# Gathering ten tiles ahead, score bursts set by the gather's position, smaller loads on more steps, and an FFN that runs on into the next batch

## The chip, the cores and the metric

The kernel runs on one core of one Trainium2 chip. The metric is the device time of one execution in microseconds: 660.77 us in the median of four runs of the kernel before (656.48 to 662.66). The engines named below are TensorE (PE; its weight loads are listed as PEld), VectorE (DVE), ScalarE (ACT), GpSimd (POOL) and SyncE (SP), which here only issues DMAs.

## The reference

Attention whose heads are mixed twice ("talking heads"), and then a feed-forward network with a squared ReLU. Batch 8, 12 heads, 448 positions, 64 values per head; the network is 768 to 2048 to 768 over all 3584 tokens. Inputs and output are float32.

```python
scores = scale * np.matmul(q, k.transpose(0, 1, 3, 2))
scores = np.einsum('bhij,hg->bgij', scores, w_pre)
attn = softmax(scores)                       # over the last axis
attn = np.einsum('bhij,hg->bgij', attn, w_post)
x = np.matmul(attn, v)                       # heads back to 768 columns
out = np.maximum(x @ w_in, 0.0) ** 2 @ w_out
```

## The kernel before

Everything is computed in bfloat16 with float32 sums. The 448 query rows of a batch are cut into 45 tiles of ten rows (the last has eight). For one tile, the scores of ten rows and twelve heads make 120 partitions by 448 keys; both head mixings are matmuls over these 120 partitions.

**Scores and the gather.** The scores of a batch are made in four blocks (12, 12, 12 and 9 tiles). A block is 128 query rows, and its tile `S` holds them row by partition: 128 x 12 heads x 448. `score_burst` (L264) makes half a block: six matmuls into six of the eight PSUM banks, then six copies into `S`, half on ScalarE (L279) and half on VectorE (L281). There are two `S` buffers, so a block's copies overwrite the block two before it. `gather` (L286) then moves ten rows from `S` into a tile `G` with 120 partitions, by a DMA that SP issues (L293). It needs the whole block, since each gather reads all heads. `G` has `AHEAD + 2` buffers.

**A step.** One tile is one step, and all batches run as one row of 360 steps (L371). In step i: `mix` (L296) multiplies `G` with the first mixing matrix (L299), ScalarE takes exp and its row sums (L302), VectorE the reciprocal (L304), and GpSimd scales to `d` (L306). `unmix` (L310) of the tile four steps back (`LAG`) does the second mixing and the transposition in four matmuls (L319), copied out by VectorE (L321). Then the gather of tile i + `AHEAD` is issued. The `exp` tile has three buffers.

**Other units on TensorE.** `turn_unit` (L133) transposes four heads of q or k of a batch and copies them to `qT` or `kT` on VectorE (L147). A batch has six such units. `bias_unit` (L153) and `av_unit` (L164) make the values' part; an `av` unit ends in three ScalarE activations (L179), and there are two for each third of a batch. A batch's feed-forward network is 16 FFN1 units (`ffn1_unit`, L207: six matmuls, ReLU on ScalarE L214, square on GpSimd L215) and 14 FFN2 units (`ffn2_unit`, L230: matmuls, a copy on VectorE for each second unit, stores issued by SP). The ReLU's tile `hr` has two buffers.

**What sets the order.** PE and POOL are under a manual schedule: their order is the order in which the loop emits. Two kinds of unit are put between the steps. Timed units stand in a table by step (`at_step`). FFN units stand in a list, `filler`. Each unit has a price in ns, written by hand. `fill(share)` is called twice in a step; it adds `share` to a balance and emits units until the balance is used up:

```python
rest = NT - (s0[1] if s0 else 0)
share = sum(w for w, _ in filler) / max(rest - 1, 1) / 2 if s0 else 1e9
...
for w, f in now:
    f()
    owed[0] -= w
fill(share)
```

So timed units are charged to the same balance. A batch's FFN units enter the list in step 5 of the next batch, and `rest` makes them end with that batch's last step; in steps 0 to 4 the list is empty. The turns of the next batch stand in steps 20 and 35, bias in step 20, `av` units in steps 20, 35 and 5 of the next batch. Score bursts of the next block stand in tile steps 0 and 4 of a block (0 and 2 of the short one).

**Loads.** GpSimd issues them (they cast to bfloat16): v, k and q of a batch as one DMA each (672 KB as landed) and each weight in four DMAs (768 KB), at steps of the table `loads`. The staging tiles of q and k have one buffer each, v has two. Only the first batch's q and k are loaded by four heads (224 KB).

**The start.** Three rounds, each of which turns four heads of k and q and makes their scores for block 0; then block 1; then the first six gathers.

Of the kernel before, what the change touches and what calls it, by code (L numbers as in the profile page):

```python
# [30 lines left out]
LAG = 4  # L31
AHEAD = 6
SCALE = 1.0 / 8.0
# [4 lines left out]
def kernel(  # L38
# [93 lines left out]

    def turn_unit(b, which, u):  # L133

        store, name = (qTs, "qT") if which == 0 else (kTs, "kT")
        if b not in store:
            store[b] = work.tile([P, NPAIR, S], BF16, name=name, tag=name, bufs=2)
        src = staged[b][which]
        ps = bank("tr_ps", BF16)
        for y in range(2):  # L140
            p = 2 * u + y
            for r in range(R):
                c = S * y + PR * r
                for hh in range(2):
                    nc.tensor.transpose(ps[64 * hh:64 * hh + 64, c:c + PR], src[0:PR, 2 * p + hh, r, :],  # L145
                                        ident[0:PR, 0:PR])
        nc.vector.tensor_copy(out=store[b][:, 2 * u:2 * u + 2, :],  # L147
                              in_=ps[:, 0:2 * S].rearrange("p (y s) -> p y s", y=2))

# [34 lines left out]

    def load_v(b):
        vs[b] = stage_tile("v", 2)
        load(vs[b], v, b)

    def load_k(b):
        kst = stage_tile("kst", 1)  # L190
        load(kst, k, b)
        staged[b] = (stage_tile("qst", 1), kst)

    def load_q(b):
        load(staged[b][0], q, b)

    def load_w1(x):
        n = DFF // 4
        nc.gpsimd.dma_start(out=w1[x][:, :, :],
                            in_=moe_w_in[:, n * x:n * x + n].rearrange("(c p) f -> p c f", p=P))  # L200

    def load_w2(x):
        n = DFF // 4
        nc.gpsimd.dma_start(out=w2[x][:, :, :],
                            in_=moe_w_out[n * x:n * x + n, :].rearrange("(c p) m -> p c m", p=P))
# [137 lines left out]
    with tc.manual_schedule(engines={PE, POOL}):  # L343
        first = turn_units(0)
        for x in range(3):
            first[2 * x][1]()
            first[2 * x + 1][1]()
            score_burst(0, 0, [2 * x, 2 * x + 1])
        for x in range(2):
# [8 lines left out]

        at_load(0, load_v, 0)
        at_load(2, load_k, 1)  # L360
        at_load(5, load_q, 1)
        for x in range(4):
            at_load(10 + 5 * x, load_w1, x)
            at_load(44 + 4 * x, load_w2, x)
        for b in range(B):
            if b + 1 < B:
                at_load(NT * b + 32, load_v, b + 1)
            if b + 2 < B:
                at_load(NT * b + 36, load_k, b + 2)
                at_load(NT * b + 40, load_q, b + 2)  # L370
        for i in range(len(steps) + LAG):  # L371
# [4 lines left out]
            if s0:  # L376
                b, t = s0
                blk, tl = divmod(t, TPB)
                if t == 0:
# [3 lines left out]
                    if b + 1 < B:  # L383
                        for x, u in enumerate(turn_units(b + 1)):
                            at_step(i + 16 + LAG if x < 3 else i + 31 + LAG, u)
            rest = NT - (s0[1] if s0 else 0)
            share = sum(w for w, _ in filler) / max(rest - 1, 1) / 2 if s0 else 1e9
            now = timed.pop(i, [])
# [14 lines left out]
            if i + AHEAD < len(steps):  # L403
                gather(steps[i + AHEAD])
            if s0:
                nxt = blocks.index((b, blk)) + 1
                first = [0, 4] if blk < 3 else [0, 2]
                if 1 < nxt < len(blocks) and tl in first:
                    x = first.index(tl)
                    score_burst(*blocks[nxt], [3 * x, 3 * x + 1, 3 * x + 2])  # L410
# [36 lines left out]
```

The softmax here doesn't subtract the row's maximum and nothing guards it: scores larger than these inputs give would overflow.

## Time and profile before

| | |
|---|---|
| median of four runs | 660.77 us |
| the profiled execution's own time | 662.66 us |
| its span, first to last instruction | 660.8 us |
| first mix / last mix (start) | 21.9 / 612.6 us |
| mean granted TensorE clock | 0.954 |
| first FFN1 unit | 109.3 us |
| last FFN, after the last mix's steps | 618.8 to 656.2 us |
| moved by DMA | 73.47 MB, of it 49.57 on the queue of SP and 22.81 on that of GpSimd |

The profile is of one execution, so sums in its durations are compared with 662.66, not with the median. A group's row gives busy time, the mean of one instruction, and then the idle time of that engine just before these instructions with what ended it. Matmuls are pipelined: the mean of one is longer than what it costs in a packed row. Idle time of an engine that isn't the bound costs nothing.

### The profile page before, as it was taken

The numbers are of one execution on the slowest core, as the hardware profiler recorded it, in microseconds if no ns is written. First come the engines' busy times: TensorE is split into PE (matmuls) and PEld (weight loads), VectorE is DVE, ScalarE is ACT, GpSimd is POOL, SyncE is SP. The second block draws the span as 40 slices with busy tenths as digits, with TensorE's granted clock in tenths as the row PEclk, the third lists the DMA queues.
The fourth block names the chain that finished last, engine by engine and source line by source line (L and its number), as shares of the span: only waits on it lengthen the run. The fifth ranks groups of instructions, "written<-read, shape, count | busy, mean of one in ns | idle before, by whom it ended". The sixth has DMA issues, their size and how long they took to land.

```text
span 660.8 us, 16952 instructions
## 1 busy us (share of the span) xinstructions
PE 606.0 (92%) x6282; PEld 375.5 (57%) x6282; DVE 422.6 (64%) x1029; ACT 405.1 (61%) x1193; POOL 374.7 (57%) x531
## 2 busy tenths in 40 slices
PE   4588758999899998999899999999899999999897
PEld 3245525666556655656556655656556665656554
DVE  3367656656676777677676778677676668665201
ACT  2567547755687548765687548765587549864330
POOL 3445456774387536774387536774377537763350
PEclk9668759999899999999999999999899999999899
DMA  9699999558744785349744695349744645433002
GB/s 127 101 190 198 164 153 196 108 73 134 162 73 80 128 141 121 73 73 152 161 88 80 120 151 126 67 73 158 162 79 72 109 96 109 77 68 95 23 0 84
DMA packets 90039, 73.47 MB, mean 111 GB/s; under 512 B 5476, under 2 KB 86884, under 8 KB 89956
## 3 DMA queue, kind: packets, MB, share of 16 engines
q1 hardware_dynamic: 51842, 49.57, 34.4%
q0 software_dynamic: 37984, 22.81, 26.0%
q8 instruction: 49, 0.80, 0.5%
q14 instruction: 34, 0.28, 0.1%
q10 hardware_dynamic: 130, 0.01, 0.0%
HBM read 45.63 MB, written 11.01 MB: 86 GB/s over the span
## 4 chain that ended last, share of the span: by engine, by line
PE 72%; DMA 17%; ACT 3%; DVE 3%; issue 2%; SPq 1%; POOL 1%; ACTq 0%; DVEq 0%; POOLq 0%
PE h_ps L210 22%; PE o_ps L237 19%; DMA G<-S 14%; PE m_ps L299 9%; PE at_ps L319 9%; PE ot_ps L171 5%; PE s_ps L274 5%; PE tr_ps L145 2%; DMA out_dram<-osb 2%; ACT e_sb L302 2%; DVE at L321 1%; SPq L293 1%; DMA qst<-in_q_dram 1%; PE vs_ps L158 1%; ACT S L279 1%
## 5 line engine op out<-in xcount | busy, mean ns | idle before, releaser
L306 POOL TENSOR_SCALAR d<-e_sb,rc 120x448 bf16<-120x448 f32 x360 | 228.4, 638 | 248.7 <-DVE rc L304 247.1
L321 DVE CAST at<-at_ps 112x480 bf16<-112x480 f32 x360 | 230.0, 651 | 99.3 <-PE at_ps L319 97.0
L302 ACT ACTIVATE e_sb<-m_ps 120x448 f32<-120x448 f32 x360 | 196.8, 555 | 130.2 <-PE m_ps L299 115.1
L299 PE MATMUL m_ps<-G,pre 120*120 120x448 bf16 x360 | 137.6, 382 | 29.9 <-DMA G<-S 25.5
L210 PE MATMUL h_ps<-xt,w 128*128 128x448 bf16 x768 | 164.7, 353 | 0.3
L237 PE MATMUL o_ps<-w,h 128*128 128x384 bf16 (+1 forms) x1024 | 162.5, 327 | 0.0
L319 PEld LDWEIGHTS <-d 120*128 120x128 bf16 (+1 forms) x1440 | 112.1, 102 | 55.4 <-issue 9.7
L319 PE MATMUL at_ps<-post,d 120*128 120x120 bf16 (+1 forms) x1440 | 139.2, 221 | 4.5 <-POOL d L306 3.7
L215 POOL TENSOR_TENSOR h<-hr 128x448 bf16<-128x448 f32 x128 | 119.2, 932 | 14.8 <-ACT hr L214 14.8
L237 PEld LDWEIGHTS <-h 128*128 128x128 bf16 (+1 forms) x1024 | 86.6, 101 | 52.4 <-issue 3.2
L210 PEld LDWEIGHTS <-w 128*128 128x128 bf16 x768 | 73.3, 98 | 60.7 <-issue 5.9
L281 DVE CAST S<-s_ps 128x448 bf16<-128x448 f32 x184 | 103.5, 616 | 4.8 <-PE s_ps L274 2.8
L279 ACT CAST S<-s_ps 128x448 bf16<-128x448 f32 x200 | 94.4, 553 | 15.7 <-PE s_ps L274 15.7
L214 ACT ACTIVATE hr<-h_ps 128x448 f32<-128x448 f32 x128 | 69.7, 544 | 47.9 <-PE h_ps L210 46.7
L304 DVE RECIPROCAL rc<-sm 120x1 f32<-120x1 f32 x360 | 56.8, 159 | 53.3 <-ACT e_sb L302 50.4
L299 PEld LDWEIGHTS <-pre 120*120 120x120 bf16 x360 | 49.1, 137 | 68.3 <-DMA G<-S 38.1
L302 ACT ACTIVATION_READ_ACCUMULATOR e_sb<-m_ps 120x1 f32 x360 | 76.7, 213 | 0.0
L179 ACT ACTIVATE xt<-ot_ps,bvec 128x150 bf16<-128x150 f32 (+1 forms) x144 | 42.9, 391 | 37.4 <-PE ot_ps L171 37.4
L274 PE MATMUL s_ps<-kT,qT 64*128 64x448 bf16 x384 | 60.3, 377 | 5.8 <-DVE qT L147 2.2
L244 DVE COPY osb<-o_ps 128x384 f32<-128x384 f32 x48 | 26.7, 557 | 51.5 <-PE o_ps L237 51.5
L171 PE MATMUL ot_ps<-at,v 112*64 112x150 bf16 x1152 | 48.2, 246 | 3.2 <-issue 2.0
L171 PEld LDWEIGHTS <-v 112*64 112x64 bf16 x1152 | 44.1, 121 | 5.6 <-issue 4.7
(33 smaller groups left out, 158.4 us busy)
## 6 DMA issues: line engine op xcount, KB each, us to landing
G<-S SPq DMA_DIRECT2D x352, 105.0 KB
v<-in_v_dram POOLq DMA_DIRECT2D x8, 672.0 KB, 10.7
kst<-in_k_dram POOLq DMA_DIRECT2D x7, 672.0 KB, 10.8
qst<-in_q_dram POOLq DMA_DIRECT2D x7, 672.0 KB, 13.6
w<-in_moe_w_in_dram POOLq DMA_DIRECT2D x4, 768.0 KB, 10.7
w<-in_moe_w_out_dram POOLq DMA_DIRECT2D x4, 768.0 KB, 10.7
out_dram<-osb SPq DMA_DIRECT2D x8, 336.0 KB
out_dram<-osb SPq DMA_DIRECT2D x8, 288.0 KB
```

What stands on the lines that cost most here:

```text
L171: nc.tensor.matmul(ps[64 * hh:64 * hh + 64, TQ * y:TQ * y + TQ], lhsT=vs[b][0:PR, g, r, :], rhs=at[0:PR, r, g, :], start=(y == 0 and r == ...
L210: nc.tensor.matmul(ps[:, 0:S], lhsT=w1[ft // 4][:, c2, ft % 4 * 128:ft % 4 * 128 + 128], rhs=xts[b][:, c2, :], start=(c2 == 0), stop=(c2 = ...
L215: nc.gpsimd.tensor_tensor(out=h2[:, :], in0=hr[:, :], in1=hr[:, :], op=ALU.mult)
L237: nc.tensor.matmul(dst, lhsT=h2ts[(b, ft)][:, mt * 128:mt * 128 + ROWS[mt]], rhs=w2[ft // 4][:, ft % 4, n2 * 384:(n2 + 1) * 384], start=(f ...
L274: nc.tensor.matmul(ps[:, 0:S], lhsT=qTs[b][rs, p, BLK_START[blk]:BLK_START[blk] + P], rhs=kTs[b][rs, p, :], start=True, stop=True)
L279: nc.scalar.copy(out=sb[:, h, :], in_=ps[:, 0:S])
L281: nc.vector.tensor_copy(out=sb[:, h, :], in_=ps[:, 0:S])
L299: nc.tensor.matmul(ps[0:n, 0:S], lhsT=pre[0:n, 0:n], rhs=Gs.pop(s)[0:n, :], start=True, stop=True)
L302: nc.scalar.activation(out=e[0:n, :], in_=ps[0:n, 0:S], func=ACT.Exp, scale=SCALE, accum_out=sm[0:n, 0:1])
L306: nc.gpsimd.tensor_scalar(out=d[0:n, 0:S], in0=e[0:n, :], scalar1=rc[0:n, 0:1], scalar2=-1.0 / S, op0=ALU.mult, op1=ALU.add)
L319: nc.tensor.matmul(ps[:, RG * r:RG * r + RG], lhsT=d[0:n, PR * r:PR * r + P], rhs=post[0:n, :], start=True, stop=True)
L321: nc.vector.tensor_copy(out=ats[(b, third)][0:PR, :, :, IQ * tl:IQ * tl + IQ], in_=ps[0:PR, 0:R * RG].rearrange("p (r g i) -> p r g i", r= ...
```

## The change

- `AHEAD` goes from 6 to 10: ten gathers before the first step, tile i + 10 in step i, and 12 `G` buffers.
- A score burst is emitted by the position of the gather, not of the mix: when the gather is at tile 2 and tile 6 of a block (2 and 5 of the short one), the next block's bursts follow. In steps, both bursts of a block come eight steps earlier than before (eight and seven where the short block precedes).
- q, k and v are loaded by four heads, the weights by half quarters, one piece a step, two steps apart or three. Batch 1's q and k come first, then v of batch 0, then the weights; batch 2's q and k partly move behind the first batch's end. From batch 1 on, q and k of the batch after next stand on steps 22 to 32 and the next v on 34 to 38.
- The turns: three now in step 16 (batch 0), 12 (batch 1) or 5 (later), the other three in step 20. At the start the copy of q goes to ScalarE, and the scores of a round are made one round later.
- `rest` now counts to step 5 of the next batch, so that FFN units are spread over 45 steps, from step 6 to step 5 of the batch after.

```diff
@@ -29,7 +29,7 @@
 TT = 15
 TQ = TT * IQ
 LAG = 4
-AHEAD = 6
+AHEAD = 10
 SCALE = 1.0 / 8.0
 ROWS = [128, 128, 128, 64]
 
@@ -130,7 +130,7 @@
                 out=cgblk[64 * hh:64 * hh + 64, :],
                 in0=ps[64 * hh:64 * hh + 64, 0:H].rearrange("p (c t) -> p t c", t=2)[:, hh, :], scalar1=1.0 / S)
 
-    def turn_unit(b, which, u):
+    def turn_unit(b, which, u, eng=None):
 
         store, name = (qTs, "qT") if which == 0 else (kTs, "kT")
         if b not in store:
@@ -144,8 +144,8 @@
                 for hh in range(2):
                     nc.tensor.transpose(ps[64 * hh:64 * hh + 64, c:c + PR], src[0:PR, 2 * p + hh, r, :],
                                         ident[0:PR, 0:PR])
-        nc.vector.tensor_copy(out=store[b][:, 2 * u:2 * u + 2, :],
-                              in_=ps[:, 0:2 * S].rearrange("p (y s) -> p y s", y=2))
+        (eng or nc.vector.tensor_copy)(out=store[b][:, 2 * u:2 * u + 2, :],
+                                       in_=ps[:, 0:2 * S].rearrange("p (y s) -> p y s", y=2))
 
     def turn_units(b):
         return [(430, lambda u=u, w=w: turn_unit(b, w, u)) for u in range(NPAIR // 2) for w in (1, 0)]
@@ -182,26 +182,30 @@
     def av_units(b, third):
         return [(800, lambda cp=cp: av_unit(b, third, cp)) for cp in range(2)]
 
-    def load_v(b):
-        vs[b] = stage_tile("v", 2)
-        load(vs[b], v, b)
-
-    def load_k(b):
-        kst = stage_tile("kst", 1)
-        load(kst, k, b)
-        staged[b] = (stage_tile("qst", 1), kst)
-
-    def load_q(b):
-        load(staged[b][0], q, b)
+    def load_v(b, x):
+        if x == 0:
+            vs[b] = stage_tile("v", 2)
+        load(vs[b], v, b, 4 * x, 4 * x + 4)
+
+    def load_qk(b, x):
+        if x == 0:
+            kst = stage_tile("kst", 1)
+            staged[b] = (stage_tile("qst", 1), kst)
+        u, w = x // 2, 1 - x % 2
+        load(staged[b][w], k if w else q, b, 4 * u, 4 * u + 4)
 
     def load_w1(x):
         n = DFF // 4
-        nc.gpsimd.dma_start(out=w1[x][:, :, :],
-                            in_=moe_w_in[:, n * x:n * x + n].rearrange("(c p) f -> p c f", p=P))
+        h = NPAIR // 2
+        c = x % 2 * h
+        nc.gpsimd.dma_start(out=w1[x // 2][:, c:c + h, :],
+                            in_=moe_w_in[128 * c:128 * c + 128 * h, n * (x // 2):n * (x // 2) + n].rearrange(
+                                "(c p) f -> p c f", p=P))
 
     def load_w2(x):
-        n = DFF // 4
-        nc.gpsimd.dma_start(out=w2[x][:, :, :],
+        n = DFF // 8
+        c = x % 2 * 2
+        nc.gpsimd.dma_start(out=w2[x // 2][:, c:c + 2, :],
                             in_=moe_w_out[n * x:n * x + n, :].rearrange("(c p) m -> p c m", p=P))
 
     def ffn1_unit(b, ft):
@@ -341,11 +345,12 @@
     blocks = [(b, blk) for b in range(B) for blk in range(4)]
     steps = [(b, t) for b in range(B) for t in range(NT)]
     with tc.manual_schedule(engines={PE, POOL}):
-        first = turn_units(0)
-        for x in range(3):
-            first[2 * x][1]()
-            first[2 * x + 1][1]()
-            score_burst(0, 0, [2 * x, 2 * x + 1])
+        for x in range(4):
+            if x < 3:
+                turn_unit(0, 1, x)
+                turn_unit(0, 0, x, nc.scalar.copy)
+            if x > 0:
+                score_burst(0, 0, [2 * x - 2, 2 * x - 1])
         for x in range(2):
             score_burst(0, 1, [3 * x, 3 * x + 1, 3 * x + 2])
         for x in range(AHEAD):
@@ -356,18 +361,22 @@
         def at_load(i, f, *args):
             loads.setdefault(i, []).append(lambda: f(*args))
 
-        at_load(0, load_v, 0)
-        at_load(2, load_k, 1)
-        at_load(5, load_q, 1)
-        for x in range(4):
-            at_load(10 + 5 * x, load_w1, x)
-            at_load(44 + 4 * x, load_w2, x)
-        for b in range(B):
+        for x in range(6):
+            at_load(2 * x, load_qk, 1, x)
+            at_load([40, 42, 44, 46, 55, 57][x], load_qk, 2, x)
+        for x in range(3):
+            at_load(12 + 2 * x, load_v, 0, x)
+            at_load(49 + 2 * x, load_v, 1, x)
+        for x in range(8):
+            at_load(18 + 3 * x, load_w1, x)
+            at_load(48 + 2 * x, load_w2, x)
+        for b in range(1, B):
+            if b + 2 < B:
+                for x in range(6):
+                    at_load(NT * b + 22 + 2 * x, load_qk, b + 2, x)
             if b + 1 < B:
-                at_load(NT * b + 32, load_v, b + 1)
-            if b + 2 < B:
-                at_load(NT * b + 36, load_k, b + 2)
-                at_load(NT * b + 40, load_q, b + 2)
+                for x in range(3):
+                    at_load(NT * b + 34 + 2 * x, load_v, b + 1, x)
         for i in range(len(steps) + LAG):
             for f in loads.get(i, []):
                 f()
@@ -382,9 +391,9 @@
                     at_step(i + 16 + LAG, (900, lambda b=b: bias_unit(b)))
                     if b + 1 < B:
                         for x, u in enumerate(turn_units(b + 1)):
-                            at_step(i + 16 + LAG if x < 3 else i + 31 + LAG, u)
-            rest = NT - (s0[1] if s0 else 0)
-            share = sum(w for w, _ in filler) / max(rest - 1, 1) / 2 if s0 else 1e9
+                            at_step(i + 16 + LAG if x >= 3 else i + {0: 16, 1: 12}.get(b, 1 + LAG), u)
+            rest = (1 + LAG - i) % NT + 1
+            share = sum(w for w, _ in filler) / rest / 2 if s0 else 1e9
             now = timed.pop(i, [])
             if s0:
                 mix(s0)
@@ -402,11 +411,12 @@
                     at_step(i + 2, (0, lambda b1=b1: filler.extend(ffn_units(b1))))
             if i + AHEAD < len(steps):
                 gather(steps[i + AHEAD])
-            if s0:
-                nxt = blocks.index((b, blk)) + 1
-                first = [0, 4] if blk < 3 else [0, 2]
-                if 1 < nxt < len(blocks) and tl in first:
-                    x = first.index(tl)
+                b2, t2 = steps[i + AHEAD]
+                blk2, tl2 = divmod(t2, TPB)
+                nxt = 4 * b2 + blk2 + 1
+                first = [2, 6] if blk2 < 3 else [2, 5]
+                if 1 < nxt < len(blocks) and tl2 in first:
+                    x = first.index(tl2)
                     score_burst(*blocks[nxt], [3 * x, 3 * x + 1, 3 * x + 2])
             if i + 1 < len(steps) + LAG:
                 fill(share)
```

## The prediction

> **What bounds the kernel now.** I read the page's busy shares and its 40 slices first, then the busy time stage by stage, one stage per batch (the stages start at the first mix of each batch).
>
> ```profile
> PE 606.0 (92%) x6282; PEld 375.5 (57%) x6282; DVE 422.6 (64%) x1029; ACT 405.1 (61%) x1193; POOL 374.7 (57%) x531
> ...
> PE   4588758999899998999899999999899999999897
> ...
> PEclk9668759999899999999999999999899999999899
> DMA  9699999558744785349744695349744645433002
> ```
> ```profile
> 21.90:85.60 63.70, 46.27 (x487) 28.07 (x487) 39.81 (x108) 39.38 (x124) 35.12 (x53) 0.75 0.96 169
> 85.60:170.60 85.00, 77.19 (x786) 47.73 (x787) 52.60 (x127) 49.97 (x146) 48.99 (x69) 0.91 0.78 140
> 320.20:394.60 74.40, 71.91 (x789) 44.96 (x787) 53.36 (x129) 49.78 (x148) 45.56 (x64) 1.00 0.62 113
> 320.17:329.66 9.49, 7.16 (x94) 4.20 (x91) 7.67 (x20) 7.66 (x24) 3.89 (x7) 1.00 0.66 164
> 329.66:349.47 19.81, 19.81 (x152) 11.48 (x149) 14.52 (x35) 16.26 (x48) 17.42 (x24) 1.00 0.46 89
> ```
>
> The columns are window, length, busy PE, PEld, DVE, ACT, POOL, then granted clock and DMA share. Batch 0 has DMA at 0.96 and the clock at 0.75; from batch 2 on TensorE is the bound, with the clock at 1.00. But a busy matmul row is not packed work, so I set a packed price for each unit from places where PE never waits:
>
> ```profile
> 329.66 0.35 PE L299 MATMUL m_ps<-G,pre 120*120 120x448 bf16 x1
> 330.06 0.35 PE L299 MATMUL m_ps<-G,pre 120*120 120x448 bf16 x1
> ```
>
> A mix plus an unmix is 0.40 us (330.06 - 329.66). The chain gives 1.14 for an FFN1 unit and 1.30 for an FFN2 unit (1.42 for the 64-row ones); a burst of six scores is 0.79, three turns 1.2, two av units 1.57, bias 0.9. Per batch: 45 x 0.40 + 16 x 1.14 + 12 x 1.30 + 2 x 1.42 + 8 x 0.79 + 2 x 1.2 + 3 x 1.57 + 0.9 = 69 us. Batch 4 takes 74.4, and batches 2 to 6 together 374.2 - 345.2 = 29 over their packed work, 5.8 each. Where? Steps 0 to 5 hold 6 x 0.40 + 2 x 0.79 + 1.57 = 5.55 us of packed work and take 9.49: 3.9 of the 5.8, here:
>
> ```profile
> 320.66 0.76 PE L274 MATMUL s_ps<-kT,qT 64*128 64x448 bf16 x6
> ...
> 323.26 0.40 PE L299 MATMUL m_ps<-G,pre 120*120 120x448 bf16 x1 [1.05 <-DMA G<-S]
> ...
> 324.33 0.40 PE L299 MATMUL m_ps<-G,pre 120*120 120x448 bf16 x1 [0.46 <-DMA G<-S]
> ...
> 326.60 0.35 PE L274 MATMUL s_ps<-kT,qT 64*128 64x448 bf16 x1 [0.43 <-ACT S L279]
> ```
>
> No FFN unit stands in these steps, so PE waits for gathers and then for evacuations. The prices for those:
>
> ```profile
> L306 POOL TENSOR_SCALAR d<-e_sb,rc 120x448 bf16<-120x448 f32 x360 | 228.4, 638 | 248.7 <-DVE rc L304 247.1
> L321 DVE CAST at<-at_ps 112x480 bf16<-112x480 f32 x360 | 230.0, 651 | 99.3 <-PE at_ps L319 97.0
> ...
> L215 POOL TENSOR_TENSOR h<-hr 128x448 bf16<-128x448 f32 x128 | 119.2, 932 | 14.8 <-ACT hr L214 14.8
> ...
> L281 DVE CAST S<-s_ps 128x448 bf16<-128x448 f32 x184 | 103.5, 616 | 4.8 <-PE s_ps L274 2.8
> ...
> L304 DVE RECIPROCAL rc<-sm 120x1 f32<-120x1 f32 x360 | 56.8, 159 | 53.3 <-ACT e_sb L302 50.4
> ```
>
> VectorE needs 0.65 + 0.16 = 0.81 a step and 3 x 0.616 = 1.85 a burst. Steps 0 to 5 cost it 6 x 0.81 + 3.7 = 8.6 against 5.55 of PE work, an excess of 3.0.
>
> The sum is made against the profiled 662.66 (span 660.8, 1.86 around it); a gain is then taken from the median of 660.77.
>
> **Steady batches (2 to 6).** Working share and owed through step by step, FFN units now stand in steps 0, 1, 3 and 4; steps 5 to 7 stay empty, because the turns and av units of step 5 are charged to owed. The same sum by place: steps 4 to 8 (two bursts, three turns, two av, two FFN2 units) give VectorE 10.2 us and PE 9.1, excess 1.1; steps 20 to 23 now hold a burst beside bias, turns and av: 7.1 against 6.1, excess 1.0. The nearest row is steps 0 to 5 of batch 7, where gathers had landed in time: excess 3.0, loss 2.1 (its mixes stand 7.62 us apart from step 0 to step 6). So about 0.7 at each of the two, 0.4 for the unfilled burst of step 41, 1.0 for small losses that stay: 2.8 of loss in place of 5.8. The gather waits go: the burst that a batch's first gathers read is done four steps ahead of the gather, where now it is one.
>
> Against it stands POOL. Six loads per batch now fall on steps 22 to 32, where FFN1 units still stand on 24 to 29, 31 and 32.
>
> ```profile
> kst<-in_k_dram POOLq DMA_DIRECT2D x7, 672.0 KB, 10.8
> ...
> kst<-in_k_dram POOLq DMA_DIRECT2D x3, 224.0 KB, 6.4
> ```
>
> A 672 KB issue held POOL 0.97 us, a 224 KB one 0.70 (timeline). Over steps 24 to 32 POOL owes 9 x 0.64 + 8 x 0.93 + 5 x 0.7 = 16.7, PE 9 x 0.40 + 8 x 1.14 + 2 x 0.79 = 14.3. Queued behind a load on POOL are d, for which exp waits three tiles on (three e buffers) and unmix four, and h, for which the relu waits two units on. Two buffers cover about 2 us; I take 1.0 a batch (0 if all is covered, 2.5 if nothing). The Trainium skill (DMA: Bandwidth & Descriptors, "Measured") speaks against this part: batch to 1 MiB or more, since each DMA has about 2 us fixed. By the rule six more DMAs cost 12 us a batch. The rows say the time to landing falls from 10.8 to 6.4, the packets stay 512 bytes, and each piece is used 8 or more steps later; so only the issue counts, 9 x 0.70 - 3 x 0.97 = 3.4 us a batch on POOL, most of it under PE. I take the rows.
>
> Gain: 5.8 - 2.8 - 1.0 = 2.0 a batch, 10 us over five (3 to 16).
>
> **Prologue.** The q copy moves to ScalarE (a 128x896 copy on VectorE 0.62; ScalarE took 0.55 for a 448-wide one, so 0.5 to 1.1), beside the k copy; but bursts 2 and 3 now wait behind turn 2. The last turn ends at 15.3 either way; two copies in parallel, then eight evacuations on two engines: first gather near 17.7 for 18.04. Gain 0.3 (-1 to 1), kept in the next sum.
>
> **The opening, to the first FFN unit.** Before, it starts in step 58, at 109; worked through, the new order puts it in step 61, with 3 steps, one burst and three turns (3.2 us of PE) more behind it. Equal would be 108.7 + 3.2 = 112.
> - A new wait: in step 4 the first burst of block 2 overwrites the S buffer of block 0, whose gather 11 is in flight. Counting packets of 896 bytes, 120 a gather, gathers 0 to 7 landed 21.2 to 28.6, one per 1.06 us: gather 11 lands at 33 to 35, the burst is reached at 26. Behind its copies on ScalarE is exp 5, on VectorE the next rc and at copies, and PE runs out of banks: about 7 us of VectorE idle. Before, PE waited 5.1 us for gather 8 in the same stretch, so half of it is not new. PE's clock falls to 0.50 in such a wait (30 to 40 us). The skill (TensorE: Matmul & The Clock Gate, Part 1) asks for some 3.4 us busy before full rate returns; that would add up to 1.7 us of matmul time, but evacuations bound this stretch, and I add nothing.
> - v0 is now loaded on steps 12 to 16 and used in step 20: landing 6.4 after issue, four steps of 1.0 to 1.2: up to 2 us of wait.
> - VectorE's floor: 61 x 0.81 + 10 x 1.85 + 9 x 0.62 = 73.5, which from 21.6 gives 95. The gathers' floor: 72 after the first, at 1.06 alone and 1.1 to 1.5 beside loads (12 to 23: 1.23): 20 + 72 x 1.23 = 109. Before, such waits made 19 us over the floor. v1, the second q and k leave batch 0 (16.5 of 16-engine time), so the pace may be better.
> - The weights' halves cost POOL eight more issues of 0.7, with POOL busy 35.12 of 63.70; they land long before steps 61 and 82, where they are first read: nothing. If POOL had no room, 5.6.
> I take 109: gain 3 (-6 to 10).
>
> **Batch 7 and end.** Its steps 0 to 5 lose 2.0, the last unmixes 4.1 with 2.0 idle; five FFN2 units now stand ahead of these. Gain 2 (0 to 4). The 4.6 us of last stores stay.
>
> Sum: 10 + 3 + 2 = 15; 662.66 - 15 = 647.7, on the median's scale 646.
>
> **The rivals.**
> 1. *Covered nothing* (0.15): POOL's 2.5 a batch is uncovered and the opening stays DMA-bound at the old pace. 15 - 5 x 1.5 - 6 = 1.5: 659 (655 to 666). For it: POOL is busy 17.42 of 19.81 in an FFN1 stretch already.
> 2. *Slower* (0.15): the S buffer. Every block's first burst now comes three steps behind the last gather that reads the buffer, before seven. SP issues the gather of tile i + 10 when mix i - 2 has freed its buffer (101 us of SP's waits end on a mix), so that gather is out some five steps ahead, 8 us, and landings took 3.3 in the median, 6.2 at the ninth tenth and 8.1 at most in batches 2 to 7: covered. If stores hold SP's queue so that it is issued in its own step, only 4.9 us are left; then ScalarE and VectorE stall 2 us in the two blocks of a batch that meet loads or stores. 7 x 4 + 8 in the opening = 36, less a gain of 20: 677. It decides from landings of over 5 us at those gathers.
> 3. *The opening set free* (0.08): gathers at 1.06 throughout, VectorE's floor plus the step-4 wait: first FFN unit near 100; gain 12 + 10 + 4 = 26: 635 or less.
>
> **How the numbers follow.** Forecast 0.62, 646 (636 to 653). The range: adding the low ends (3 - 6 + 0) gives 664, the upper ends 631. 632 to 665 leaves out most of rival 2 and a little at the bottom. About 1% is what a measurement tells from no change: faster (below 654) 0.62 + 0.08, less 0.01 at the forecast's upper end, = 0.69; same 0.15 + 0.01 = 0.16, slower 0.15.
>
> **What would show it.** Right: no FFN-less wait for gathers in steps 0 to 3, batches of 72 to 73 us with PE over 0.97 busy, first FFN1 unit near 109. POOL right: e waiting for d, or hr for h, in steps 24 to 32. Wrong if "S copy waits for DMA G" appears with over 1 us a block (rival 2), if batches 2 to 6 stay at 74 or more (rival 1), or if the first FFN unit comes by 101 (rival 3) or after 118.

## The result, and the profile after

| | before | after |
|---|---|---|
| median | 662.73 us (64 runs, 656.34 to 673.88) | 657.88 us (43 runs, 655.71 to 660.39) |
| the profiled execution's own time | 662.66 us | 659.26 us |
| its span | 660.8 us | 657.2 us |
| start of the first mix of batch 0 / 1 / 2 / 7 | 21.9 / 85.6 / 170.6 / 544.8 us | 21.3 / 88.6 / 170.6 / 538.0 us |
| first FFN1 unit | 109.3 us | 115.7 us |

The ratio of after to before is 0.994, with a 95% interval of 0.9926 to 0.9954; it leaves out the runs that were over 1.5% above the fastest of their kernel, which the medians of the table do not. The change saves some 4 us of 660; the forecast was 15. (The runs of before made beside the later experiments put its median 2 us above the 660.77 that the prediction started from.)

The windows of the changed kernel, one per batch for batches 0, 1, 4 and 6, show where it went. Columns: window, length, busy PE, PEld, DVE, ACT, POOL, then granted clock, DMA share and GB/s.

```profile
21.30:88.60 67.30, 46.50 (x498) 28.41 (x499) 40.15 (x108) 40.82 (x127) 38.60 (x60) 0.75 0.85 153
88.60:170.60 82.00, 70.17 (x724) 42.60 (x722) 52.75 (x131) 50.78 (x152) 61.97 (x90) 0.92 0.94 161
319.10:392.70 73.60, 71.28 (x790) 44.81 (x787) 53.12 (x128) 49.76 (x148) 48.93 (x71) 1.00 0.66 114
466.30:537.90 71.60, 70.56 (x788) 44.89 (x786) 53.16 (x128) 49.51 (x148) 44.66 (x65) 1.00 0.55 98
```

Batch 0 got longer: 67.3 us, where it took 63.7. Its DMA share fell from 0.96 to 0.85, so the engines that move the opening's loads stood idle part of the time, although batches 0 and 1 together load the same tiles. Batch 1 looks shorter (82.0 for 85.0), but TensorE has less to do in it: 70.17 us busy for 77.19, since part of the first FFN is carried into batch 2. The steady batches got shorter, and they are not alike: batch 4 takes 73.6, and batch 6, which has no loads of q and k, takes 71.6.

With the packed prices of the prediction, the time that each stretch loses over its packed work can be set side by side. This is the whole result (us; batches 0 and 1 have 97.5 us of packed work before and 91.0 after):

| stretch | lost before | lost after | gain | forecast |
|---|---|---|---|---|
| prologue, to the first mix (its length) | 21.9 | 21.3 | 0.6 | 0.3 |
| batches 0 and 1 | 51.2 | 58.3 | -7.1 | 3, with the prologue |
| batches 2 to 6 | 29.0 | 20.8 | 8.2 | 10 |
| batch 7 and the end | 7.2 | 5.3 | 1.9 | 2 |
| sum | | | 3.6 | 15 |

The sum agrees with the difference of the spans, 660.8 - 657.2 = 3.6. So three of four terms were near, and the opening swallowed their gain.

**What the opening waits for.** In the view of waits, up to 125 us, ScalarE and VectorE show a row that the kernel before has almost not (for its whole span: VectorE 0.5 us, ScalarE none). Columns: total us, times, longest.

```profile
ACT S L283 <- DMA G<-S: 13.4, 4, 4.6
```
```profile
DVE S L285 <- DMA G<-S: 10.4, 4, 4.3
```

These are the copies of a score burst into `S` that wait until a gather has read the block two before from the same buffer. The timeline at the first of them (step 4's burst; TensorE is in step 7 when it has to stand) shows who stands behind:

```profile
29.13 1.25 POOL L310 TENSOR_SCALAR d<-e_sb,rc 120x448 bf16<-120x448 f32 x2
...
34.41 1.84 ACT L283 CAST S<-s_ps 128x448 bf16<-128x448 f32 x4 [4.28 <-DMA G<-S]
34.47 1.16 DVE L285 CAST S<-s_ps 128x448 bf16<-128x448 f32 x2 [3.98 <-DMA G<-S]
34.99 0.56 PE L323 MATMUL at_ps<-post,d 120*128 120x120 bf16 x4 [4.03 <-ACT S L283]
...
35.79 0.63 POOL L310 TENSOR_SCALAR d<-e_sb,rc 120x448 bf16<-120x448 f32 x1 [4.73 <-DVE rc L308]
```

From 31.1 to 34.4 us no engine computes. ScalarE's next exp and VectorE's next reciprocal are queued behind the copies, TensorE waits for the bank that ScalarE's copy is to free, GpSimd for the reciprocal. The same wait of ScalarE ends again at 47 us (2.0), at 82 us (4.6) and at 115 us (2.6).

These waits stand in the place of others. TensorE's waits for the gathers themselves are largely gone from the opening: before, up to 170 us (all of them before 110),

```profile
PE m_ps L299 <- DMA G<-S: 20.5, 15, 5.1
```

and after, up to 125 us,

```profile
PE m_ps L303 <- ACT S L283: 6.5, 2, 4.5
...
PE m_ps L303 <- DMA G<-S: 4.9, 5, 2.6
PE at_ps L323 <- ACT S L283: 4.0, 1, 4.0
PE s_ps L278 <- ACT S L283: 3.7, 2, 3.4
...
PE h_ps L214 <- ACT S L283: 2.0, 1, 2.0
```

So 15.6 us of waiting for gathers went, and 16.2 us of waiting for ScalarE's `S` copies came, which had themselves waited 13.4 us for gathers.

The second loss is in the loads. Counted from the trace's DMA packet records, by 80 us the queue of GpSimd had moved 7.75 MB before and 5.86 MB after, of the 11.8 MB that the opening needs (the last of it landed at 119.9 and 133.3 us). The first reason is in GpSimd's waits of the same stretch:

```profile
POOL kst L70 <- PE tr_ps L145: 7.2, 1, 7.2
```

The first load in the loop is now k of batch 1, which must wait for the transposes to free the one staging tile; v, which had a free buffer and was issued at step 0, comes at step 12 (42.7 us, for 6.7 before).

**The steady batches.** Steps 0 to 3 now lose nothing; the 1.05 and 0.46 us waits for gathers are gone, as forecast. What is left is at steps 24 to 34, where GpSimd's timeline in batch 4 reads:

```profile
361.85 0.92 POOL L219 TENSOR_TENSOR h<-hr 128x448 bf16<-128x448 f32 x1
362.72 0.76 POOL L70 DMA_DIRECT2D kst<-in_k_dram  x1
363.52 0.64 POOL L310 TENSOR_SCALAR d<-e_sb,rc 120x448 bf16<-120x448 f32 x1
364.13 0.93 POOL L219 TENSOR_TENSOR h<-hr 128x448 bf16<-128x448 f32 x1
365.04 0.63 POOL L310 TENSOR_SCALAR d<-e_sb,rc 120x448 bf16<-120x448 f32 x1
365.65 0.92 POOL L219 TENSOR_TENSOR h<-hr 128x448 bf16<-128x448 f32 x1
366.52 0.75 POOL L70 DMA_DIRECT2D qst<-in_q_dram  x1
```

There is no gap: GpSimd sets the pace here. Its load issues hold it 0.75 us each. Over the whole execution ScalarE's relu waits 16 times for GpSimd's square, a row that the kernel before doesn't have:

```profile
ACT hr L218 <- POOL h L219: 13.3, 16, 1.3
```

The busy time of GpSimd over the span went from 374.7 to 405.0 us.

### The profile page after: what moved, and what is told of

Same layout as the page of the kernel before. It is cut to its first block, busy times and chain, and to the rows that moved or that the text cites. A ratio compares the mean times of both kernels' runs of the same rounds, so it can differ in the third digit from the quotient of the medians.

```text
span 657.2 us, 17021 instructions
## 1 busy us (share of the span) xinstructions
PE 596.6 (91%) x6282; PEld 371.4 (57%) x6282; DVE 419.2 (64%) x1026; ACT 405.6 (62%) x1196; POOL 405.0 (62%) x583
## 4 chain that ended last, share of the span: by engine, by line
PE 62%; POOL 15%; DMA 9%; issue 5%; ACT 5%; DVE 2%; SPq 1%; ACTq 0%; DVEq 0%; POOLq 0%
PE o_ps L241 21%; PE h_ps L214 15%; PE at_ps L323 8%; PE m_ps L303 8%; DMA G<-S 7%; POOL d L310 7%; POOL h L219 5%; PE ot_ps L171 5%; PE s_ps L278 3%; ACT S L283 2%; PE tr_ps L145 2%; POOL qst L70 1%; POOL kst L70 1%; DVE S L285 1%; ACT e_sb L306 1%
## 5 line engine op out<-in xcount | busy, mean ns | idle before, releaser
L303 PE MATMUL m_ps<-G,pre 120*120 120x448 bf16 x360 | 132.5, 368 | 17.9 <-ACT S L283 9.6
L323 PEld LDWEIGHTS <-d 120*128 120x128 bf16 (+1 forms) x1440 | 106.5, 100 | 73.2 <-issue 19.3
L323 PE MATMUL at_ps<-post,d 120*128 120x120 bf16 (+1 forms) x1440 | 137.2, 219 | 11.5 <-POOL d L310 6.1
L283 ACT CAST S<-s_ps 128x448 bf16<-128x448 f32 x200 | 93.6, 554 | 34.4 <-PE s_ps L278 17.8
L214 PEld LDWEIGHTS <-w 128*128 128x128 bf16 x768 | 73.1, 98 | 69.1 <-issue 15.6
L306 ACT ACTIVATION_READ_ACCUMULATOR e_sb<-m_ps 120x1 f32 x360 | 78.2, 217 | 0.0
L179 ACT ACTIVATE xt<-ot_ps,bvec 128x150 bf16<-128x150 f32 (+1 forms) x144 | 42.7, 392 | 40.0 <-PE ot_ps L171 40.0
L278 PE MATMUL s_ps<-kT,qT 64*128 64x448 bf16 x384 | 55.8, 372 | 5.8 <-ACT S L283 3.7
L171 PE MATMUL ot_ps<-at,v 112*64 112x150 bf16 x1152 | 46.0, 240 | 3.5 <-DVE at L325 3.5
L171 PEld LDWEIGHTS <-v 112*64 112x64 bf16 x1152 | 42.3, 117 | 6.8 <-issue 6.7
```

The lines of the kernel that those rows point to most:

```text
L171: nc.tensor.matmul(ps[64 * hh:64 * hh + 64, TQ * y:TQ * y + TQ], lhsT=vs[b][0:PR, g, r, :], rhs=at[0:PR, r, g, :], start=(y == 0 and r == ...
L214: nc.tensor.matmul(ps[:, 0:S], lhsT=w1[ft // 4][:, c2, ft % 4 * 128:ft % 4 * 128 + 128], rhs=xts[b][:, c2, :], start=(c2 == 0), stop=(c2 = ...
L278: nc.tensor.matmul(ps[:, 0:S], lhsT=qTs[b][rs, p, BLK_START[blk]:BLK_START[blk] + P], rhs=kTs[b][rs, p, :], start=True, stop=True)
L283: nc.scalar.copy(out=sb[:, h, :], in_=ps[:, 0:S])
L303: nc.tensor.matmul(ps[0:n, 0:S], lhsT=pre[0:n, 0:n], rhs=Gs.pop(s)[0:n, :], start=True, stop=True)
L306: nc.scalar.activation(out=e[0:n, :], in_=ps[0:n, 0:S], func=ACT.Exp, scale=SCALE, accum_out=sm[0:n, 0:1])
```

## The experiments

Two theories stood at the start for the opening. *S*: the reuse of the two `S` buffers. *L*: the new load schedule. For the steady batches: the *place* of the loads among the FFN1 units, against their *number*. Each kernel was timed beside the kernel before on the same chip; all ratios are to the kernel before. The mark by which the opening is read is the start of batch 2 in the profiled execution: 170.6 both before and after, though after has 6.5 us less packed work ahead of it.

**1. Bursts later.** The changed kernel with its score bursts three steps later, so that a block's copies come further behind the gathers:

```diff
-                first = [2, 6] if blk2 < 3 else [2, 5]
+                first = [5, 8] if blk2 < 3 else [4, 6]
```

> The changed kernel with one edit: the bursts follow the gather at tiles 5 and 8 of a block (4 and 6 of the short one) in place of 2 and 6 (2 and 5), so that the first copy into an S buffer stands eight steps, not five, behind the last gather that reads it. Theory S (the opening lost its gain because the first S copies of blocks wait for gathers, five times up to the first FFN units, 16 us of idle PE in the trace of the changed kernel): three more steps of 0.8 us or more take 2.4 us or more off each wait, 8 to 12 us in all, and the steady batches stay at 73.6: 646 to 650. Theory L (the piecewise loads did it, by holding GpSimd and by bringing v late): no change, 656 to 660.

Measured: 657.12 us, ratio 0.989 (0.9815 to 0.9965); batch 2 starts at 169.7. This seemed to speak for L, but it is a weak test: the waits of ScalarE on gathers were still 10.2 us (13.4 without the edit), since three steps of the opening are only two or three microseconds. The steady batches took 72.9 us for 73.6, which was not followed up. Batch 1 did start 1.3 us earlier (87.3); then TensorE's turns in step 20 of batch 1 waited 2.8 us for k and 4.4 us for q of batch 2, which in the changed kernel they don't.

**2. The old loads.** The changed kernel with the load functions and load steps of before.

```diff
-        for x in range(6):
-            at_load(2 * x, load_qk, 1, x)
...
+        at_load(0, load_v, 0)
+        at_load(2, load_k, 1)
+        at_load(5, load_q, 1)
...
```

> The changed kernel with the loads of the kernel before: whole tiles and quarters at their old steps; gathers, bursts, turns and FFN spread as changed. Theory S: the S waits of the opening stay (16 us), the opening ends no earlier; but no load falls on FFN1 steps any more, so batches 1 to 5 go from 73.6 to the 71.6 that batch 6 (which has no such loads) takes: about 10 us less, 648. Theory L: the same, and the opening comes back by 7 to 10 us as well: 638 to 641.

Measured: 652.66 us, ratio 0.9814 (0.9748 to 0.9879). All of the gain is in the steady batches (71.6 us each); batch 2 starts at 170.8. In the opening taking L away gained nothing, because the other wait grew. ScalarE's waits up to 125 us:

```profile
ACT S L279 <- DMA G<-S: 27.3, 3, 11.1
```

**3. A third S buffer.** The changed kernel with three; to make room it has one `G` and one `osb` buffer less.

```diff
-            Sb[(b, blk)] = work.tile([P, H, S], BF16, name="S", tag="S", bufs=2)
+            Sb[(b, blk)] = work.tile([P, H, S], BF16, name="S", tag="S", bufs=3)
...
```

> The changed kernel with three S buffers in place of two, so that a block's copies wait for no gather at all; to make room G has 11 buffers in place of 12 and the output tile osb one in place of two. Theory S: all five waits of the opening go, 14 to 16 us less if the gathers then keep up, some 8 if they become the bound; the single output tile may cost 0 to 5 us in the FFN2 steps of later batches: 642 to 652. Theory L: 656 to 662.

Measured: 657.35 us, ratio 0.9891 (0.9827 to 0.9956); batch 2 starts at 169.1. The waits of `S` copies for gathers are gone from ScalarE's rows, and batch 1 starts 6.3 us earlier (82.4 for 88.65). Then the gain is lost in one step, step 20 of batch 1, which lasts 15.7 us where it took 5.1. The timeline there:

```profile
117.29 0.96 PE L145 MATMUL tr_ps<-ident,kst 112*64 112x112 bf16 x16 [3.32 <-DMA kst<-in_k_dram]
...
122.40 0.96 PE L145 MATMUL tr_ps<-ident,qst 112*64 112x112 bf16 x16 [4.14 <-DMA qst<-in_q_dram]
```

The turns of batch 2 wait for q and k, whose last pieces are issued in steps 55 and 57 among the halves of the second weight. So taking S away alone gains little either (1.6 us). Experiments 2 and 3 together look like two theories refuted; the other reading is that there are two causes in series, each late enough to hide the removal of the other.

**4. The FFN carried over, alone.** The kernel before with two lines of the change:

```diff
-            rest = NT - (s0[1] if s0 else 0)
-            share = sum(w for w, _ in filler) / max(rest - 1, 1) / 2 if s0 else 1e9
+            rest = (1 + LAG - i) % NT + 1
+            share = sum(w for w, _ in filler) / rest / 2 if s0 else 1e9
```

> The kernel before with the new rest and share alone: FFN units spread up to step 5 of the next batch; loads, gathers, bursts and turns as before. If the gain in the steady batches comes from FFN units in steps 0 to 4, it is here without the price of the loads on FFN1 steps: batches 2 to 6 from 74.8 to 71.6 to 72.5, the end 2 us earlier, the opening as before: 643 to 650. If the ten tiles ahead are needed for it (gather waits of the batch's start stay and only move FFN units behind them): batches at 74 or more, 656 to 662.

Measured: 652.67 us, ratio 0.9822 (0.9757 to 0.9888), between the two expectations. These two lines alone beat the whole change. Batches 2 to 6 take 366 us for 374. TensorE still waits 4.0 us for gathers after the start of batch 2 (5.0 before the edit), so it is the idle place in steps 0 to 5 that is filled, not the gathers that come sooner. So this part of the steady gain needs no deeper gathers. It is about half of what there is: experiment 2, which has the same loads and also the deeper gathers, with the bursts and turns that go with them, takes 359.2 us for the five batches. Batch 2 starts at 164.4; with the 8 us of FFN work that this kernel carries over, its first two batches lose 53 us over their packed work, nearly the 51.2 of before.

**5. Loads off the FFN1 steps.** The changed kernel; the nine pieces per batch stay, eleven steps later:

```diff
-                    at_load(NT * b + 22 + 2 * x, load_qk, b + 2, x)
+                    at_load(NT * b + 33 + 2 * x, load_qk, b + 2, x)
...
-                    at_load(NT * b + 34 + 2 * x, load_v, b + 1, x)
+                    at_load(NT * b + 45 + 2 * x, load_v, b + 1, x)
```

> The changed kernel with two edits of the steady loads alone: q and k of the batch after next on steps 33 to 43 in place of 22 to 32, the next v on steps 0 to 4 of its own batch in place of 34 to 38 of the one before, so that none of them stands among FFN1 units; nine pieces a batch stay. If it is the place of the pieces beside FFN1 units that costs 2.0 us a batch (73.6 against 71.6), batches 2 to 5 come to 71.6 with as many DMAs, and the whole to 648 to 650. If it is their number, batches stay at 73 to 73.6: 655 to 658.

Measured: 646.80 us, ratio 0.9767 (0.9714 to 0.982): place, not number. The windows of batches 4 and 5:

```profile
311.16:382.69 71.53, 70.64 (x789) 44.82 (x786) 53.28 (x128) 49.55 (x148) 48.79 (x71) 1.00 0.68 118
382.69:454.31 71.62, 70.59 (x789) 44.92 (x786) 53.26 (x128) 49.43 (x148) 48.76 (x71) 1.00 0.67 115
```

GpSimd is as busy as before the edit (48.8 against 48.9), with the same 71 instructions, and the batch is 2.0 us shorter. Batch 2 also starts 4 us earlier (166.7). Half of these are in batch 0, which the edit doesn't touch: the start of batch 2 can differ by some 2 us with no edit to account for it, and differences of that size in the start of batch 2 are not read below.

**6. Both causes away.** Experiments 2 and 3 in one kernel: old loads and three `S` buffers. Here "D" is the theory of two causes in series.

> The changed kernel with the loads of the kernel before and with three S buffers (G 11, output tile one). Theory D (the opening is bound by what the DMA engines must land before step 65: with two S buffers the copies wait for gathers behind the loads, with three and the piecewise loads the wait moved to q, k and v of step 65, since the pieces left DMA idle early and queue behind half of the second weights): old loads keep DMA busy from the start and the weights come last, so both waits go, batch 2 begins at 158 to 163 in place of 170, and the whole is 638 to 643. If the S buffer alone matters as in the run with three buffers and piecewise loads: 645 to 650. If neither: 652 to 653 as with old loads alone.

Measured: 642.37 us, ratio 0.9711 (0.9647 to 0.9776). Batch 2 starts at 158.9, 11.7 us ahead of the changed kernel, where each edit alone gave 0 to 1.6. In the terms of the table of losses, batches 0 and 1 now lose 46.5 us: the opening gains 4.7 where the change lost 7.1. The ScalarE row on gathers is absent; TensorE's waits up to 125 us are now for the gathers themselves and for the first k:

```profile
PE m_ps L299 <- DMA G<-S: 15.5, 12, 3.8
PE tr_ps L145 <- DMA kst<-in_k_dram: 7.7, 2, 6.3
PE at_ps L319 <- POOL d L306: 2.6, 4, 0.9
```

**7. The small pieces in the order of need.** Is it the pieces or their order? The changed kernel with experiment 5, three `S` buffers, and the same pieces issued in the order in which they are used:

```diff
-            at_load(2 * x, load_qk, 1, x)
-            at_load([40, 42, 44, 46, 55, 57][x], load_qk, 2, x)
+            at_load(2 + 2 * x, load_qk, 1, x)
+            at_load(28 + 2 * x, load_qk, 2, x)
...
-            at_load(12 + 2 * x, load_v, 0, x)
-            at_load(49 + 2 * x, load_v, 1, x)
+            at_load(0, load_v, 0, x)
+            at_load(40 + 2 * x, load_v, 1, x)
...
-            at_load(18 + 3 * x, load_w1, x)
-            at_load(48 + 2 * x, load_w2, x)
+            at_load(13 + 2 * x, load_w1, x)
+            at_load(46 + 2 * x, load_w2, x)
```

> The changed kernel with three S buffers (G 11, output tile one), loads off FFN1 steps in the steady batches, and the pieces of the opening in the order of need and without gaps: v of batch 0 at step 0, q and k of batch 1 on steps 2 to 12, first weights 13 to 27, q and k of batch 2 on 28 to 38, v of batch 1 on 40 to 44, second weights 46 to 60. Theory D: no wait at step 65, batch 2 begins at 158 to 163, whole 638 to 643. If pieces themselves are what costs in the opening (GpSimd held, gathers delayed): batch 2 begins at 168 or later, 646 to 650.

Measured: 646.03 us, ratio 0.9746 (0.9682 to 0.9809). The opening did better than expected (batch 2 at 155.7, the earliest of all; 7.84 MB loaded by 80 us), the whole worse by 3. In the terms of the table of losses, batches 0 and 1 lose 43.3 us. The steady batches pay for the memory (72.6 to 73.3 us for the 71.6 of experiment 5): with one `osb` buffer VectorE waits for the stores, in the waits from 155 to 620 us:

```profile
DVE osb L248 <- DMA out_dram<-osb: 37.2, 13, 4.0
```

**8. Gathers ahead, alone.** The kernel before with `AHEAD` 10, the bursts by the gather's position, and the moved turns; loads and FFN shares as before.

```diff
-AHEAD = 6
+AHEAD = 10
...
+                first = [2, 6] if blk2 < 3 else [2, 5]
+                if 1 < nxt < len(blocks) and tl2 in first:
...
-                            at_step(i + 16 + LAG if x < 3 else i + 31 + LAG, u)
+                            at_step(i + 16 + LAG if x >= 3 else i + {0: 16, 1: 12}.get(b, 1 + LAG), u)
```

> The kernel before with ten tiles ahead, the bursts tied to the gather and the turns at the changed steps; loads, FFN spread and start as before. The S waits of the opening come here too, as long as with old loads (8 to 11 us each, three of them, partly in place of old waits): batch 2 begins 4 to 8 us later than the 170.6 before. Steady batches lose their gather waits but not the empty steps 0 to 4: 72.5 to 74 for 74.8. Sum: 655 to 665. If instead gathering ahead is what fills the batch's start: batches at 72 or less and 645 to 650.

Measured: 676.04 us, ratio 1.0197 (1.0125 to 1.0269), more than was expected. This is the time of the prediction's second rival (677), on this part alone. Two thirds of it are in the opening: batch 2 starts at 180.7, 10 us late. ScalarE's and TensorE's waits up to 125 us:

```profile
ACT S L279 <- DMA G<-S: 29.2, 3, 11.6
```
```profile
PE at_ps L319 <- ACT S L279: 17.2, 2, 9.0
PE s_ps L274 <- ACT S L279: 8.6, 1, 8.6
```

The other 6 us are in batches 2 to 6 (380.5 us for 374.2), and the trace shows the same wait there. Without FFN units steps 0 to 2 of a batch take 0.4 us each, so step 4's burst reaches its buffer early: in each of the five batches `S` copies wait there for a gather or a store, and TensorE waits for ScalarE's copies, 1.6, 2.3, 0.8, 1.8 and 3.6 us. So in the steady batches gathers ahead (with their bursts and turns) alone cost 6 us, the carried FFN alone gains 8 (experiment 4), and both together, with the same loads, gain 15 (experiment 2): FFN work in steps 0 to 4 is also what gives the gathers time.

**9. Order of need with two S buffers.** Experiment 7 without the third `S` buffer, so also with both `osb` buffers and the twelfth `G` buffer.

```diff
-            Sb[(b, blk)] = work.tile([P, H, S], BF16, name="S", tag="S", bufs=3)
+            Sb[(b, blk)] = work.tile([P, H, S], BF16, name="S", tag="S", bufs=2)
...
```

> As the run with the pieces in the order of need, but with the two S buffers (and G 12, output tile two) of the changed kernel: the fourth field of a two by two of S buffers and load order. Start of batch 2 so far: 166.7 us with two buffers and the changed opening, 169.1 with three; 170.8 with two buffers and old loads, 158.9 with three; 155.7 with three and the pieces in order. If the two causes stand in series (each hides the other's removal), the S waits come back here: batch 2 at 163 to 168, later batches at 71.6: 643 to 647. If the order of loads was enough by itself: 156 to 159, whole 635 to 638.

Measured: 647.51 us, ratio 0.9772 (0.972 to 0.9824). Batch 2 starts at 169.1 again, a little later than the 163 to 168 expected, and TensorE stands behind the S copies:

```profile
PE s_ps L278 <- ACT S L283: 10.2, 2, 7.3
```

With it the table of the start of batch 2 is complete:

| opening's loads | two `S` buffers | three |
|---|---|---|
| as changed | 170.65 (166.7 with experiment 5) | 169.1 |
| in order of need, small pieces | 169.1 | 155.7 |
| of before, whole tiles | 170.8 | 158.9 |

From the changed kernel, either the loads or the third buffer alone moves it by 4 us at most; both together by 12 to 15. (The kernels of the third column also have one `G` and one `osb` buffer less, and those of the second row contain experiment 5.)

**10 and 11. Order and size of the loads, with room.** Three `S` buffers paid for by `AHEAD` 8 with nine `G` buffers, and with the last rows' store using the same two `osb` buffers as the others. Experiment 10 has the pieces of experiment 7, experiment 11 the whole tiles of before.

```diff
-AHEAD = 10
+AHEAD = 8
...
-        g = work.tile([P, S], BF16, name="G", tag="G", bufs=AHEAD + 2)
+        g = work.tile([P, S], BF16, name="G", tag="G", bufs=AHEAD + 1)
...
-            osb = ffnp.tile([P, 384], F32, name="osb3", tag="osb3", bufs=1)
+            osb = ffnp.tile([P, DMODEL], F32, name="osb", tag="osb", bufs=2)
```

> A version meant to be the fastest: pieces in the order of need, off FFN1 steps, three S buffers, and two output tiles again; the room comes from eight tiles ahead with nine G buffers and from the last rows sharing the output tile. Opening as in the run in order with three buffers (batch 2 at 155 to 159), and batches of 71.6 in place of the 72.6 to 73.3 that the single output tile gave: profile 634 to 637, median 636 to 641.

> The same room and three S buffers with the loads of the kernel before (16 whole-tile and quarter DMAs less than a third as many as the pieces). If pieces are worth something once their place is right: 2 to 4 us slower than the version in order, all of it before batch 2. If the order alone counts: the same within 1.5 us, 636 to 641.

Measured: 642.28 us, ratio 0.9689 (0.9644 to 0.9734), and 641.14 us, ratio 0.9663 (0.9612 to 0.9713), the one 1.3 us above the expected band, the other at its upper edge; batch 2 starts at 160.2 and 158.1. Why experiment 10 starts it 4.5 us later than experiment 7, with the same pieces, was not followed up. The intervals overlap: once order and place are right, 224 KB or 672 KB a piece is not to be told apart. The steady batches take 71.9 us in both. Both beat the kernel before and the changed kernel; the second has the lowest median of all, though experiments 6 and 10 are not told apart from it.

## Why the prediction was wrong

**The failed step: the opening, and in it the cover of the S buffer.** The forecast was a gain of 3 (-6 to 10); measured is a loss of 6.5 with the prologue counted in, 7.1 without, just outside the low end. The mechanism had been seen: "A new wait: in step 4 the first burst of block 2 overwrites the S buffer of block 0". This first wait was sized well: gather 11 was to land at 33 to 35 us, and the copies went on at 34.4. It even cost nothing net, since TensorE had waited 5.1 us for a gather in the same step before (mix 12 starts at 39.4 us before, 39.6 after).

What failed is that the wait was counted once, and its recurrence dismissed in rival 2: "that gather is out some five steps ahead, 8 us ... covered", against landings of 3.3 us in the median and 8.1 at most. At the four waits of ScalarE the last gather that reads the buffer (gathers 11, 23, 44 and 68) had been issued only 1.4, 3.6, 6.0 and 6.5 us before the copies' turn came, and the copies went on 5.7, 5.6, 10.5 and 9.1 us after its issue; 13.4 us of waiting in all. Five steps are 8 us in a steady batch, where a step holds FFN work and lasts 1.6 us. In the opening there is no FFN; a step that waits for nothing lasts about 0.8 us (steps 5 and 6 with three `S` buffers: 0.82 and 0.77). SP, moreover, took 1.0 us to issue a gather (gathers 0 to 11 left one behind the other from 17.5 to 28.7 us), so gather 11, which stands in step 1, left when TensorE was in step 5. Steady steps were set against steady landings, and the answer was carried to a stage where both are different. In the steady batches the judgement held: over the whole execution ScalarE has no wait of this kind beyond these four.

**The opening's loads.** The prediction had "v1, the second q and k leave batch 0 ... so the pace may be better". The pace was worse, because work that leaves batch 0 must be done before step 65, and the DMA engines had idle time instead: a share of 0.74 from 20 to 40 us (0.89 before), and 5.86 MB loaded by 80 us in place of 7.75. Experiment 3 shows what is late next when the S wait is away, q and k of batch 2. How much of this cause is the late v, how much the wait for the staging tile and how much the place of the second weight was not separated; experiment 7 changed all of them at once. The bound "half weights: nothing" missed that their issues also stand in steps without FFN. There d and a load take turns on GpSimd and set the step, 1.37 us, as its timeline at 107 us shows (up to 125 us TensorE waits 6.1 us for d, where it waited 2.8 before):

```profile
107.68 0.75 POOL L70 DMA_DIRECT2D kst<-in_k_dram  x1
...
108.46 0.65 POOL L310 TENSOR_SCALAR d<-e_sb,rc 120x448 bf16<-120x448 f32 x1
109.05 0.74 POOL L208 DMA_DIRECT2D w<-in_moe_w_out_dram  x1
...
109.84 0.65 POOL L310 TENSOR_SCALAR d<-e_sb,rc 120x448 bf16<-120x448 f32 x1
110.42 0.75 POOL L70 DMA_DIRECT2D qst<-in_q_dram  x1
```

**First FFN1 unit.** Forecast 109 in step 61; the step was right (its mix is at 110.8), the unit came at 115.7, behind one more S wait of 2.6 us. This lay between "near 109" and the "after 118" that was named as refuting.

**Steady batches, mechanism right.** The forecast per batch was 2.8 of loss plus 1.0 for GpSimd. The first term measured 2.6 (batch 6, and experiment 5's batches). GpSimd's was mis-sized: 2.0, in the four batches that load q and k, within its bounds of 0 to 2.5. The demand had been worked out, 16.7 against 14.3 us, an excess of 2.4; that two buffers would absorb half of it was the mistake. A shortage that lasts eight steps can use up two buffers only once, which fits the 2.0; no run varied the number of buffers. v's three pieces on steps 34 to 38 cost nothing: batch 6 has them. On the rule of large transfers (the Trainium skill, DMA: Bandwidth & Descriptors, "Measured") the rows were the better guide than the 12 us a batch that was worked out from it: the six further DMAs cost 2.0 us a batch among FFN1 units, and nothing eleven steps later (experiment 5). What counted was the issue's place in GpSimd's queue.

**The small terms.** Prologue 0.6 for 0.3, the end 1.9 for 2. v0 was to cost up to 2 us: TensorE's wait for v was 2.0 up to 125 us. That the clock adds nothing held in the mean (0.75 in batch 0 before and after).

**The rivals.** The terms' own low and high ends gave 664 and 631, and the measured time lies between them; the stated 636 to 653 was narrower than its terms. The time fell on that of rival 1 (659), but not for its reason: the change did take 8.2 of the steady loss. Its price for GpSimd, 2.5 us a batch with nothing covered, measured 2.0. Rival 2 had the right mechanism, placed in the wrong stage; experiment 8 shows its price when nothing else is gained, and that its wait does come in the steady batches where no carried FFN units lengthen steps 0 to 4. The gain that the forecast put in the opening existed too: with both causes away it is 4.7 or 7.9 us (experiments 6 and 7).

## What to carry to other kernels

Before a prefetch is made deeper, count the buffers of its *source* too: producing a block earlier means overwriting the older one earlier, and the cover must be worked out in the time of the shortest steps, not of the steady ones. When undoing either of two suspected parts changes nothing, undo both before dropping either; here each hid the other, and together they were worth 12 us or more. A load issued by an engine that also computes should be placed where that engine has slack: the same nine pieces cost 2 us or nothing.

## What was not expected of the hardware

- The issue of a casting load held GpSimd 0.73 to 0.75 us in the median for 224 KB of q, k or v and 0.97 to 0.99 for 672 KB: three times the bytes cost 1.3 times the queue. For the first and the second weight it was 0.81 and 0.74 us for 384 KB, 0.87 and 0.79 for 768 KB, so it doesn't go by bytes alone.
- A gather behind whole-tile loads can be later than one behind small pieces. Gather 11, issued at 28 to 30 us, landed 9.3 and 9.6 us after its issue with loads of 672 KB (experiments 2 and 8) and 5.4 and 5.7 us with 224 KB (the changed kernel and experiment 9). The longest S waits were 11.1 and 11.6 us against 4.6 and 7.1; with the pieces packed closer (experiment 9) gather 35 took 10.7 us as well. That it is the bytes queued ahead was argued from this order, not measured by itself.
- By the packet records up to 120 us, a packet of a load (512 bytes) took 63 to 65 ns and one of a gather (896 bytes) 53 to 59 ns in the mean, in each of the thirteen kernels. So the time of a packet hardly changed with the schedule; how busy the DMA engines were early did (0.74 and 0.89 of the time from 20 to 40 us, after and before).
